# A new plan for a list-scheduled kernel: ScalarE durations from measurement, two row operations on either engine, dummy matmuls in TensorE's gaps

## Chip, cores, metric

One core of a Trainium2 chip. The metric is device microseconds of one execution, median of several runs; a trace's span is about 1.9 us shorter than the time of the same execution (284.2 and 286.15, for one). Engines: PE is TensorE, ACT is ScalarE, DVE is VectorE, POOL is GpSimd, SP issues most DMAs.

## The reference, cut

```python
def _A_ref(q, k, v, shift_k, ssm_k, ssm_D):      # q is layernorm(A_q)
    k_shift = sum(k_pad[:, t:t+S, :] * shift_k[:, ks-1-t] for t in range(ks))   # 4 taps
    kv = k_shift * v
    y = irfft2(rfft2(kv, padded to 2S) * rfft2(ssm_k, padded))[:S]   # causal convolution, length 2048
    return q * (y + kv * ssm_D)
def _B_ref(x, w_gate, w_up, w_down):
    return (silu(x @ w_gate) * (x @ w_up)) @ w_down
x = A_q                                           # [1, 2048, 640], F = 1728
h = x + _A_ref(layernorm(x), A_k, A_v, ...)
return h + _B_ref(layernorm(h), ...)
```

## The kernel before

The sequence is cut into four blocks of 512 rows. For each block, C0 to C3 is the convolution part (taps and gate on DVE, a transform on PE, products with the kernel's transforms G0 to G3 on DVE, the inverse on PE, layernorm on ACT and DVE) and F0 to F3 the FFN. The FFN of block i runs while DVE and ACT prepare block i+1. Every operation is recorded with its engine, a planned duration and what it reads and writes. A list scheduler then fixes the order of each engine's instructions; they are emitted in that order, so the planned times decide nothing but order, engine and buffer. In the views, `ps` is a buffer that matmuls write, and an eviction copies a result out of it (`wgu<-ps`); a statistic sums a row or its squares for a layernorm (`junk<-wk`, `junk<-h`). DELTA is a table of priority offsets, one for each kind of operation.

```python
DELTA = {"C0 ACT half": 5713, "C0 ACT lnh0": 1462, ...}      # 72 entries, cut
def c_act(n): return 0.09 + 0.00078 * n                       # planned ACT time: 0.59 for 640, 1.09 for 1280
def c_mm(n):  return {512: 0.217, 320: 0.137, 128: 0.107}[n]
...
# in Plan.schedule(), for the best ready operation o on engine e, startable at st:
            if e == "PE":
                if st - clock[e] > 2.0:
                    cold = st + 2.6
                if st < cold:                                  # matmuls take twice as long for a while
                    o.dur = 2 * o.dur if ...
...
pl.op("ACT", c_act(2 * D), ... nc.scalar.mul(x.t[:, 2], x.t[:, 2], 0.5), name="half",
      alt=[("DVE", c_ts(2 * D), ...)])                         # halving of a sum lane
pl.op("ACT", c_act(D), ... nc.scalar.activation(h, x, Identity, bias=-mean), name="z",
      alt=[("DVE", 0.356, ...)] if i in LN_EITHER else [])     # LN_EITHER = (0,)
act(c_act(D), ... nc.scalar.activation(hn, h, Identity, bias=..., scale=...), name="hn")   # scaled row, blocks 1 to 3
...
    order = pl.schedule()
    with tc.manual_schedule():
        for o in order:
            o.fn()
```

## Time and profile before

| | before |
|---|---|
| median time | 295.8 us (3 runs, 295.55 to 296.09) |
| span of the trace | 295.6 us |
| busy: PE, DVE, ACT | 259.5, 217.6, 213.3 us |
| first matmul of FFN0 | 68.29 us |
| first matmul of FFN3 | 244.55 us |
| end of the last matmul | 289.3 us |

A busy PE is not PE at its peak, since the ends of pipelined matmuls are modelled; how far the starts of equal matmuls lie apart tells its speed. The prediction below shows views of this trace. To one of its lines a remark: the 4.9 us wait of L809 carries the name of an ACT instruction, but its matmuls read what the gate writes, and the gate ends at 58.7, just before they start:

```profile
57.25 1.48 DVE L775 TENSOR_TENSOR wk<-wk,wk 128x2560 bf16<-128x2560 bf16 x1
```

### The profile page before, as it was taken

The page shows a single profiled execution, that of the slowest core. Times are in us where ns is not written, and L with a number is a line of the kernel's source. Part 1 is how long each engine was busy: PE and PEld are TensorE (multiplying, and loading weights), DVE is VectorE, ACT ScalarE, POOL GpSimd, SP SyncE. Part 2 cuts the span into 40 slices and gives each one's busy share as a digit, 9 for nine tenths or more (in the row PEclk, how much of TensorE's full clock was granted, in tenths as well). Part 3 has the DMA queues.
Part 4 walks back from the last instruction along what each step waited for, and adds up shares of the span by engine and source line. Part 5 has one row for each costly group of instructions (what it writes and reads, how often), then busy time and mean ns, then how long its engine had stood idle before and what let it go on. Part 6 is the DMA issues. An engine that isn't in the chain of part 4 may idle for free.

```text
span 295.6 us, 4242 instructions
## 1 busy us (share of the span) xinstructions
PE 259.5 (88%) x1551; PEld 150.9 (51%) x1564; DVE 217.6 (74%) x300; ACT 213.3 (72%) x377; POOL 31.1 (11%) x38
## 2 busy tenths in 40 slices
PE   3179998388999999899998997999999989999991
PEld 1146766154445576654444665654446754444670
DVE  6994999989989899989998999389999101121111
ACT  3687999979995968998557999962665973545321
POOL 2002001230102023011000030200000011000000
PEclk9999999959999999999999999999999999999998
DMA  7996158992994599935638698864563053550011
GB/s 237 343 376 226 44 232 252 372 385 99 292 347 114 166 351 385 380 112 143 157 71 223 241 323 310 310 214 128 119 173 94 2 133 100 146 133 0 2 44 44
DMA packets 59157, 57.82 MB, mean 196 GB/s; under 512 B 17729, under 2 KB 53762, under 8 KB 59138
## 3 DMA queue, kind: packets, MB, share of 16 engines
q1 hardware_dynamic: 57342, 47.08, 52.3%
q0 software_dynamic: 1792, 10.49, 9.3%
q8 instruction: 12, 0.20, 0.3%
q14 instruction: 7, 0.06, 0.0%
q10 hardware_dynamic: 4, 0.01, 0.0%
HBM read 45.76 MB, written 10.49 MB: 190 GB/s over the span
## 4 chain that ended last, share of the span: by engine, by line
ACT 35%; PE 30%; issue 19%; DVE 7%; DMA 5%; POOL 1%; SPq 1%; POOLq 0%; ACTq 0%; DVEq 0%
PE ps L1009 15%; ACT junk L838 6%; ACT lane L437 5%; PE ps L1033 5%; ACT junk L840 5%; PE ps L792 3%; PE ps L736 3%; ACT s L921 3%; PE ps L809 3%; ACT s L905 3%; DMA wk<-in_A_q_dram 3%; ACT sg L1013 2%; ACT uc L1014 2%; DMA lane<-xd 2%; ACT lane L745 2%
## 5 line engine op out<-in xcount | busy, mean ns | idle before, releaser
L1009 PE MATMUL ps<-hlnT,wgu 128*128 128x512 bf16 x527 | 118.3, 379 | 2.7 <-ACT uc L1014 1.1
L1009 PEld LDWEIGHTS <-wgu 128*128 128x128 bf16 x540 | 52.6, 98 | 66.1 <-issue 4.6
L1013 ACT ACTIVATE sg<-ps 128x512 bf16<-128x512 f32 (+1 forms) x56 | 33.6, 599 | 43.9 <-PE ps L1009 25.4
L1033 PE MATMUL ps<-wdA,tT 128*128 128x320 bf16 x384 | 55.6, 299 | 0.1
L1033 PEld LDWEIGHTS <-tT 128*128 128x128 bf16 x448 | 43.8, 98 | 17.4 <-issue 0.4
L1016 DVE TENSOR_TENSOR tT<-sg,uc 128x512 bf16<-128x512 bf16 (+1 forms) x56 | 22.7, 420 | 38.2 <-ACT uc L1014 38.1
L854 POOL TENSOR_TENSOR mv<-mv,mhalf 128x2 f32<-128x2 f32 (+1 forms) x12 | 18.6, 1551 | 147.2 <-DVE mv L850 81.3
L1014 ACT CAST uc<-ps 128x512 bf16<-128x512 f32 (+1 forms) x56 | 32.7, 584 | 0.3 <-PE ps L1009 0.2
L437 ACT CAST lane<-ps 128x640 bf16<-128x640 f32 x42 | 27.2, 746 | 0.9 <-PE ps L792 0.9
L736 PE MATMUL ps<-wgu,gb_t 128*128 128x320 bf16 x128 | 23.0, 318 | 3.6 <-ACT wgu L672 2.5
L1122 DVE TENSOR_TENSOR lane<-lane,lane 128x3840 bf16<-128x3840 bf16 x12 | 25.8, 2153 | 0.4 <-DMA lane<-xd 0.2
L769 DVE TENSOR_TENSOR wk<-krun,w 128x2560 bf16<-128x2560 bf16 (+1 forms) x20 | 24.0, 1218 | 0.2 <-PE ps L809 0.2
L809 PE MATMUL ps<-wk,cs_t 128*128 128x320 bf16 x96 | 17.3, 326 | 6.8 <-ACT junk L838 4.9
L1038 ACT ACTIVATE o<-ps,mean 128x640 bf16<-128x640 f32 x16 | 12.5, 786 | 14.4 <-PE ps L1033 14.4
L901 PE MATMUL ps<-eo,ci_t 128*128 128x320 bf16 x128 | 18.7, 299 | 1.6 <-DMA wgu<-in_B_w_up_dram 1.0
L736 PEld LDWEIGHTS <-gb_t 128*128 128x128 bf16 x128 | 13.1, 102 | 11.4 <-issue 4.2
L774 DVE TENSOR_TENSOR wk<-wk,wk 128x2560 bf16<-128x2560 bf16 (+1 forms) x15 | 18.0, 1217 | 0.0
L809 PEld LDWEIGHTS <-cs_t 128*128 128x128 bf16 x96 | 9.8, 104 | 12.4 <-DVE wk L775 5.2
L901 PEld LDWEIGHTS <-ci_t 128*128 128x128 bf16 x128 | 12.5, 98 | 7.0 <-issue 1.9
L838 ACT ACTIVATE junk<-wk 128x640 bf16<-128x640 bf16 x16 | 11.9, 747 | 4.6 <-DMA wk<-in_A_q_dram 4.4
L905 ACT ACTIVATE s<-ps,one,mv 128x640 bf16<-128x640 f32 x15 | 13.3, 921 | 1.8 <-POOL mv L854 0.9
L838 ACT ACTIVATE junk<-h 128x640 bf16<-128x640 bf16 x16 | 12.0, 748 | 2.1 <-DVE h L909 1.7
(94 smaller groups left out, 311.9 us busy)
## 6 DMA issues: line engine op xcount, KB each, us to landing
wgu<-in_B_w_gate_dram SPq DMA_DIRECT2D x24, 320.0 KB, 3.4
wgu<-in_B_w_up_dram SPq DMA_DIRECT2D x24, 320.0 KB, 4.3
lane<-xd SPq DMA_DIRECT2D x6, 960.0 KB, 5.5
lane<-hd SPq DMA_DIRECT2D x6, 960.0 KB, 7.9
xd<-lane POOLq DMA_DIRECT2D x4, 960.0 KB, 5.0
hd<-lane POOLq DMA_DIRECT2D x4, 960.0 KB, 6.8
krun<-in_A_k_dram SPq DMA_DIRECT2D x4, 640.0 KB, 6.8
wk<-in_A_v_dram SPq DMA_DIRECT2D x4, 640.0 KB, 8.7
```

Source lines behind the costliest of these rows:

```text
L437: nc.scalar.copy(dst(), src())
L736: nc.tensor.matmul(ps.t[:, h, 0:NH], wt, mv, start=(k == 0), stop=(k == len(ks) - 1))
L769: nc.vector.tensor_mul(dst.t[:, sl, :], ks, w4.t[:, j:j + 1, :].broadcast_to([P, n, D]))
L809: nc.tensor.matmul(ps.t[:, h, 0:NH], cs_t.t[:, s, n, c * P:(c + 1) * P], kv.t[:, s, h * NH:(h + 1) * NH], start=(a == 0), stop=(a == 1))
L838: act(0.73, lambda s=s: nc.scalar.activation(junk.t[:], x.t[:, s, :], ACT.Identity, scale=-1.0 / D, accum_out=mv.t[:, s:s + 1]), [(x, 1 << ...
L901: nc.tensor.matmul(ps.t[:, hh, 0:NH], ci_t.t[:, c, 1 - n, s, :], x.t[:, 2 * pos[n] + c, hh * NH:(hh + 1) * NH], start=(k == 0), stop=(k == 3))
L1009: nc.tensor.matmul(q(ps.t[:, k, 0:w]), wg.t[:, kt, off:off + P], rr(hT.t[:, kt, :]), start=(kt == 0), stop=(kt == NDC - 1))
L1013: act(c_act(w) + 0.02, lambda ps=ps, sg=sg, np_=np_, w=w: nc.scalar.activation(sg.t[0:np_, 0:w], ps.t[0:np_, 0, 0:w], ACT.Silu), [(ps, 1)] ...
L1014: act(c_act(w), lambda ps=ps, uc=uc, np_=np_, lo=up_lo, k=len(offs) - 1, w=w: nc.scalar.copy(uc.t[0:np_, 0:w], ps.t[lo:lo + np_, k, 0:w]), ...
L1016: dve(c_tt(w), lambda sg=sg, uc=uc, c=c, np_=np_, w=w, rr=rr, q=q: nc.vector.tensor_mul(rr(tv()[0:np_, c, :]), q(sg.t[0:np_, 0:w]), q(uc.t ...
L1033: nc.tensor.matmul(ps.t[:, hh, 0:NH], tv()[:, c, m * P:(m + 1) * P], wdc(c)[:, hh * NH:(hh + 1) * NH], start=(c == 0 and not oadd), stop=( ...
L1122: dve(c_tt(6 * D), lambda xl=xl, hl=hl: nc.vector.tensor_mul(xl.t[:], xl.t[:], hl.t[:]), [xl(), hl()], [xl()], name="prod")
```

## The change

Its intent: plan with ACT durations as measured, let the scheduler put two kinds of row operations on either engine in all blocks, fill planned PE gaps after the first 5.5 us with dummy matmuls so that the clock stays up, and use a table of priorities made for that plan.

```diff
-DELTA = {...72 entries...}
+DELTA = {...other entries and values...}
-OPT = (True, (0, 1, 2), (0,), ...)
+OPT = (True, (0, 1, 2), (0, 1, 2, 3), ...)          # LN_EITHER: "z" on either engine in all blocks
             if e == "PE":
-                if st - clock[e] > 2.0:
-                    cold = st + 2.6
+                lo = max(min(since[0], st), clock[e])   # since: when a PSUM buffer is free
+                if lo - clock[e] > 2.5:
+                    cold = st + 4.5
+                gap = st - 0.4 - lo
+                if st < 5.5 or st - clock[e] < 0.8 or gap < 0.3:
+                    o.warm = None
+                else:
+                    slow = min(gap, 5.5) if lo < 6.5 or lo - clock[e] > 2.5 else 0
+                    o.warm = (slots["ps"][since[1]][0], int(slow / 0.44 + (gap - slow) / 0.22))
# durations: half 1.09 -> 1.17, z 0.59 -> 0.72, y 0.59 -> 0.77, hn 0.59 -> 0.812,
#            hT 1.09 -> 1.12, down 0.59 -> 0.677; some DVE ones too
-                    act(c_act(D), ... name="hn")
+                    act(0.812, ... name="hn",
+                        alt=[("DVE", 0.357, ... nc.vector.tensor_scalar(hn, h, mean, rstd, op0=ALU.add, op1=ALU.mult))])
         for o in order:
+            if o.warm:
+                for _ in range(o.warm[1]):
+                    nc.tensor.matmul(o.warm[0][:, 0, :], ones1.t[:], ones1.t[:].unsqueeze(1).broadcast_to([P, 4, P]), start=True, stop=True)
             o.fn()
```

More of the change, by code (lines that the diff above doesn't have):

```diff
@@ L30 @@
 DELTA = {
-    "C0 ACT half": 5713,
-    "C0 ACT lnh0": 1462,
-    "C0 ACT y": 1339,
-    "C0 ACT z": -2549,
-    "C0 DVE eo0": -2261,
-    "C0 DVE gate": -16818,
-    "C0 DVE prod0": -14678,
-    "C0 DVE tinyx": 31,
-    "C0 PE inv0": -2297,
-    "C0 SP ci_t": 16022,
-    "C0 SP cs_t": 3931,
-    "C0 SP gb_t": 1107,
-    "C0 SP k": -728,
-    "C0 SP v": -11,
-    "C0 SP x": -2141,
-    "C1 ACT hn": 2424,
-    "C1 ACT xev1": -969,
-    "C1 ACT y": -4984,
-    "C1 DVE bfly0": -24238,
-    "C1 DVE bfly1": -22972,
@@ L51 @@
-    "C1 DVE eo0": -3933,
-    "C1 DVE eo1": -21519,
-    "C1 DVE hmul0": -24066,
-    "C1 DVE hmul1": -17335,
-    "C1 DVE join0": -4523,
-    "C1 DVE last": -3933,
-    "C1 DVE nm": -14579,
-    "C1 DVE prod": 733,
-    "C1 DVE tinyh1": -3279,
-    "C1 DVE xsum0": -3000,
-    "C1 PE hTtr": -11983,
-    "C2 ACT hn": -6262,
-    "C2 DVE eo0": -12365,
-    "C2 DVE eo1": -13863,
-    "C2 DVE gate": -18349,
-    "C2 DVE hmul0": -4317,
-    "C2 DVE join0": -14364,
-    "C2 DVE last": -99,
-    "C2 DVE nm": 22411,
@@ L70 @@
-    "C2 DVE prod": -4774,
-    "C2 DVE tinyx": -180,
-    "C2 DVE xsum0": -668,
-    "C2 DVE xsum1": -2435,
-    "C3 ACT hn": -8326,
-    "C3 ACT lnh0": 10,
-    "C3 ACT lnh1": -9704,
-    "C3 DVE bfly1": 20,
-    "C3 DVE comb": 3729,
-    "C3 DVE psum": -4522,
-    "C3 DVE shift": 2173,
-    "C3 DVE xsum1": 3949,
-    "C3 PE x1": -26875,
-    "C3 SP ldX": -5040,
-    "F0 DVE ffn": -3823,
-    "F0 PE down": 1944,
-    "F0 SP w": 1894,
-    "F1 PE down": 3501,
-    "F2 DVE ffn": 2826,
-    "G0 ACT gev": -234,
@@ L90 @@
-    "G0 DVE g_fold": -2452,
-    "G0 DVE skip": -2446,
-    "G0 PE g_transform": -10973,
-    "G1 ACT gev": 13784,
-    "G1 ACT half": 1293,
-    "G1 DVE g_fold": -5018,
-    "G2 ACT gev": 14649,
-    "G2 DVE g_sum": 2060,
-    "G2 PE g_turn_pe": 6402,
-    "G3 DVE g_fold": -1695,
-    "G3 DVE g_sum": 2144,
-    "G3 PE g_transform": -6565,
-    "slack SP": 3733,
+    "C0 ACT half": 860,
+    "C0 ACT lnx": 4481,
+    "C0 ACT z": 3190,
+    "C0 DVE comb": -22511,
+    "C0 DVE eo0": -12858,
+    "C0 DVE g_sum": -1393,
@@ new lines @@
+    "C0 DVE gate": -4264,
+    "C0 DVE hmul1": -12868,
+    "C0 DVE hn": -12782,
+    "C0 DVE prod0": -22408,
+    "C0 DVE shift": 4071,
+    "C0 DVE tinyx": -13190,
+    "C0 DVE xsum1": -22414,
+    "C0 SP gst": -15574,
+    "C0 SP k": -29642,
+    "C0 SP v": -16164,
+    "C0 SP x": -16163,
+    "C1 ACT lnh1": 10,
+    "C1 ACT xev0": 2001,
+    "C1 DVE bfly1": -35167,
+    "C1 DVE comb": -5098,
+    "C1 DVE eo0": -5103,
+    "C1 DVE gate": -13467,
+    "C1 DVE hmul0": -29485,
+    "C1 DVE last": -35177,
@@ new lines @@
+    "C1 DVE shift": -13857,
+    "C1 DVE tinyx": -4494,
+    "C1 DVE xsum0": -31182,
+    "C2 ACT lnh0": 1661,
+    "C2 DVE bfly1": -26086,
+    "C2 DVE hmul0": -23662,
+    "C2 DVE join1": -23656,
+    "C2 DVE shift": 177,
+    "C2 DVE tinyh0": -1588,
+    "C2 DVE tinyh1": -2274,
+    "C2 POOL powh0": -1915,
+    "C2 SP ldH": 3496,
+    "C3 ACT lnx": -2040,
+    "C3 ACT y": -2113,
+    "C3 DVE bfly0": -280,
+    "C3 DVE bfly1": -277,
+    "C3 DVE comb": -307,
+    "C3 DVE join0": -8105,
+    "C3 DVE last": -307,
@@ new lines @@
+    "C3 DVE prod": -331,
+    "C3 DVE psum": -1636,
+    "C3 DVE xsum0": -283,
+    "C3 DVE xsum1": -612,
+    "F0 ACT down": 826,
+    "F0 ACT ffn": -95114,
+    "F0 DVE ffn": -4711,
+    "F1 ACT down": -17057,
+    "F1 PE down": 8902,
+    "F2 ACT down": 993,
+    "F2 ACT ffn": -5061,
+    "F2 DVE ffn": -177,
+    "G0 ACT turn": -3610,
+    "G0 PE g_transform": -610,
+    "G1 ACT half": -914,
+    "G1 DVE g_sum": -12920,
+    "G1 SP gst": 4770,
+    "G2 ACT gev": 1247,
+    "G2 ACT half": -34281,
@@ L103 @@
+    "G2 DVE g_fold": -1451,
+    "G2 DVE g_sum": 1031,
+    "G2 PE g_turn_pe": 11630,
+    "G3 ACT half": -11180,
+    "G3 DVE g_fold": -27113,
+    "G3 DVE g_sum": -2044,
+    "G3 PE g_transform": -94287,
+    "slack ACT": 4,
+    "slack SP": 954,
 }
-OPT = (True, (0, 1, 2), (0,), (), (0, 1, 2), (1, 2, 3), True, (0,), (0,), 0, (0, 1, 2))
+OPT = (True, (0, 1, 2), (0, 1, 2, 3), (), (0, 1, 2), (1, 2, 3), True, (0,), (0,), 0, (0, 1, 2))
 def bf(a):
@@ L175 @@
 class Op:
-    __slots__ = ("i", "eng", "dur", "fn", "deps", "succ", "allocs", "frees", "pri", "nwait", "ready", "soft", "alts", "key", "start", "end", "tag", "nbytes", "fix")
+    __slots__ = ("i", "eng", "dur", "fn", "deps", "succ", "allocs", "frees", "pri", "nwait", "ready", "soft", "alts", "key", "start", "end", "tag", "nbytes", "fix", "warm")
 class Plan:
@@ L213, in op @@
         o.pri += DELTA.get(o.key, 0)
-        o.deps, o.succ, o.soft, o.allocs, o.frees = set(), [], [], [], []
+        o.deps, o.succ, o.soft, o.allocs, o.frees, o.warm = set(), [], [], [], [], None
         for x, wr in [(x, False) for x in r] + [(x, True) for x in w] + [((b, 0), True) for b in alloc]:
@@ L297, in schedule @@
             o.eng, o.dur, o.fn = next(x for x in o.alts if x[0] == e)
+            since = min(free["ps"], default=(st, 0))
             for b in o.allocs:
@@ L744, in g_sum @@
             dve(c_tt(2 * D), lambda x=x: nc.vector.tensor_add(x.t[:, 2], x.t[:, 0], x.t[:, 1]), [x(15)], [x(48)])
-            pl.op("ACT", c_act(2 * D), lambda x=x: nc.scalar.mul(x.t[:, 2], x.t[:, 2], 0.5), [x(48)], [x(48)], name="half",
+            pl.op("ACT", 1.17, lambda x=x: nc.scalar.mul(x.t[:, 2], x.t[:, 2], 0.5), [x(48)], [x(48)], name="half",
                   alt=[("DVE", c_ts(2 * D), lambda x=x: nc.vector.tensor_scalar_mul(x.t[:, 2], x.t[:, 2], 0.5))])
@@ L886, in back @@
         for s in range(NS):
-            pl.op("ACT", c_act(D), lambda s=s: nc.scalar.activation(h.t[:, s, :], xt.t[:, s, :], ACT.Identity, bias=mvx.t[:, s:s + 1]),
+            pl.op("ACT", 0.72, lambda s=s: nc.scalar.activation(h.t[:, s, :], xt.t[:, s, :], ACT.Identity, bias=mvx.t[:, s:s + 1]),
                   [(xt, 1 << s), (mvx, 1 << s)], [(h, 1 << s)],
-                  alt=[("DVE", 0.356, lambda s=s: nc.vector.tensor_scalar_add(h.t[:, s, :], xt.t[:, s, :], mvx.t[:, s:s + 1]))] if i in LN_EITHER else [], name="z")
+                  alt=[("DVE", 0.296, lambda s=s: nc.vector.tensor_scalar_add(h.t[:, s, :], xt.t[:, s, :], mvx.t[:, s:s + 1]))] if i in LN_EITHER else [], name="z")
         mvs = []
@@ L903, in back @@
                 pe(8 * c_mm(320), mm, [ci_t, (src[r][0], 15)], [ps], alloc=[y], name=f"inv{r}")
-                pl.op("ACT", c_act(D), lambda y=y, a=a, s=s, ps=ps: nc.scalar.activation(v2(y.t[:, a, :]), r3(ps.t), ACT.Identity, bias=one.t[:], scale=mvx.t[:, NS + s:NS + s + 1]),
+                pl.op("ACT", 0.77, lambda y=y, a=a, s=s, ps=ps: nc.scalar.activation(v2(y.t[:, a, :]), r3(ps.t), ACT.Identity, bias=one.t[:], scale=mvx.t[:, NS + s:NS + s + 1]),
                       [ps, one, (mvx, 16 << s)], [(y, 1 << a)],
-                      alt=[("DVE", 0.74, lambda y=y, a=a, s=s, ps=ps: nc.vector.tensor_scalar(v2(y.t[:, a, :]), r3(ps.t), mvx.t[:, NS + s:NS + s + 1], 1.0, op0=ALU.mult, op1=ALU.add))] if i == 0 else [], name="y")
+                      alt=[("DVE", 0.8, lambda y=y, a=a, s=s, ps=ps: nc.vector.tensor_scalar(v2(y.t[:, a, :]), r3(ps.t), mvx.t[:, NS + s:NS + s + 1], 1.0, op0=ALU.mult, op1=ALU.add))] if i == 0 else [], name="y")
             sl, m = slice(r, NS, 2), 5 << r
@@ L916, in nm @@
                     nc.vector.tensor_mul(mv.t[:, 3 * NS + r:4 * NS:2], mv.t[:, r:NS:2], mv.t[:, NS + r:2 * NS:2])
-                dve(0.13, nm, [(mvs[r], 5 * 17 << r)], [(mvs[r], 5 * 4096 << r)], name="nm")
+                dve(0.08, nm, [(mvs[r], 5 * 17 << r)], [(mvs[r], 5 * 4096 << r)], name="nm")
             for a in range(2):
@@ L920, in back @@
                 if i in HN_ACT:
-                    act(c_act(D), lambda hn=hn, a=a, s=s, mv=mvs[r]: nc.scalar.activation(hn.t[:, a, :], h.t[:, s, :], ACT.Identity, bias=mv.t[:, 3 * NS + s:3 * NS + s + 1], scale=mv.t[:, NS + s:NS + s + 1]),
-                        [(h, 1 << s), (mvs[r], 4112 << s)], [(hn, 1 << a)], name="hn")
+                    act(0.812, lambda hn=hn, a=a, s=s, mv=mvs[r]: nc.scalar.activation(hn.t[:, a, :], h.t[:, s, :], ACT.Identity, bias=mv.t[:, 3 * NS + s:3 * NS + s + 1], scale=mv.t[:, NS + s:NS + s + 1]),
+                        [(h, 1 << s), (mvs[r], 4113 << s)], [(hn, 1 << a)], name="hn",
+                        alt=[("DVE", 0.357, lambda hn=hn, a=a, s=s, mv=mvs[r]: nc.vector.tensor_scalar(hn.t[:, a, :], h.t[:, s, :], mv.t[:, s:s + 1], mv.t[:, NS + s:NS + s + 1],
+                                                                                                     op0=ALU.add, op1=ALU.mult))])
                 else:
@@ L943, in turned @@
                     return ps.t[:].bitcast(BF16)[:, :, 0:D].rearrange("p a (k t) -> p a k t", k=NDC)
-                pl.op("ACT", c_act(2 * D), lambda dst=dst, src=turned: nc.scalar.copy(dst(), src()), [ps], [(hT, 5 << r)],
-                      alt=[("DVE", 0.8, lambda dst=dst, src=turned: nc.vector.tensor_copy(dst(), src()))], name="hT")
+                pl.op("ACT", 1.12, lambda dst=dst, src=turned: nc.scalar.copy(dst(), src()), [ps], [(hT, 5 << r)],
+                      alt=[("DVE", 0.742, lambda dst=dst, src=turned: nc.vector.tensor_copy(dst(), src()))], name="hT")
         return h, hT
@@ L1037, in ffn @@
                 with pl.at(EVAC[i]):
-                    act(c_act(D), lambda ps=ps, m=m: nc.scalar.activation(v2(o.t[:, m, :]), r3(ps.t), ACT.Identity, bias=mean[f"x{i}"].t[:, m:m + 1]), [ps, mean[f"x{i}"]], [(o, 1 << m)], name="down")
+                    act(0.677, lambda ps=ps, m=m: nc.scalar.activation(v2(o.t[:, m, :]), r3(ps.t), ACT.Identity, bias=mean[f"x{i}"].t[:, m:m + 1]), [ps, mean[f"x{i}"]], [(o, 1 << m)], name="down")
             with pl.at(EVAC[i]):
```

## The prediction

> **What bounds the kernel now.** I first read the busy time by stretch, cut where TensorE (PE) changes its character.
>
> ```profile
> 13.80:18.20 4.40, 2.32 (x21) 2.12 (x22) 4.37 (x8) 4.31 (x10) 0.00 (x0) 1.00 1.12 341
> 18.20:24.20 6.00, 6.00 (x24) 3.33 (x24) 4.16 (x11) 4.05 (x5) 0.00 (x0) 1.00 1.05 395
> 24.30:53.90 29.60, 27.84 (x218) 19.33 (x215) 27.40 (x36) 28.26 (x39) 3.86 (x5) 1.00 0.56 187
> 53.90:68.30 14.40, 8.48 (x54) 5.47 (x54) 12.84 (x17) 12.42 (x24) 4.37 (x2) 0.76 0.95 346
> 68.30:245.30 177.00, 168.56 (x991) 95.95 (x1001) 149.98 (x195) 139.77 (x259) 19.74 (x22) 1.00 0.66 203
> 245.30:289.40 44.10, 43.82 (x243) 23.65 (x242) 6.76 (x15) 17.56 (x32) 0.69 (x2) 1.00 0.27 71
> ```
>
> After the stretch and its length come PE, weight loads, VectorE (DVE), ScalarE (ACT) and GpSimd, then the clock and the DMA share. From 68.3 us, where the first FFN (FFN0) starts, PE is the bound: its idle pieces in the timeline to 289.3 add to 7.4 us. Before that it is not: from 24 to 68 us ACT and DVE are both about 90% busy (28.26 and 27.40 of 29.6, then 12.42 and 12.84 of 14.4), and PE waits. After 289.3 come 6.3 us of eviction, add and store, which the change leaves alone.
>
> Next the waits of PE, and the timeline, for how fast its matmuls ran.
>
> ```profile
> PE ps L670 <- DVE wk L702: 8.8, 1, 8.8
> PE ps L809 <- ACT junk L838: 4.9, 1, 4.9
> PE ps L736 <- ACT wgu L672: 2.5, 2, 2.1
> ```
>
> ```profile
> 18.95 0.74 PE L736 MATMUL ps<-wgu,gb_t 128*128 128x320 bf16 x2
> 19.48 0.47 PE L736 MATMUL ps<-o,ones 128*128 128x320 bf16 x1
> ...
> 25.42 2.34 PE L736 MATMUL ps<-wgu,gb_t 128*128 128x320 bf16 x16
> ...
> 60.88 3.36 PE L809 MATMUL ps<-wk,cs_t 128*128 128x320 bf16 x12 [0.84 <-ACT lane L437]
> ```
>
> Three matmuls every 0.80 us at 19 us is 0.27 us each; sixteen in 2.2 us at 25.4 is 0.136. PE runs at half speed until about 24 us, and again from 58.8 to about 65, after the 4.9 us hole. (The clock column shows 1.00 in the first stretch, so there the durations are the evidence.)
>
> A floor follows from the counts and warm pitches of the timeline. From FFN0's first matmul on PE owes 540 matmuls of 512 columns at 0.223 us (29.30 us for 132), 664 of 320 columns at 0.137 and 40 transposes at 0.06: 120.2 + 91.0 + 2.4 = 213.6 us. The span is then 68.3 (start of FFN0) + 213.6 + 7.4 (gaps) + 6.3 (tail) = 295.6, as measured. The 213.6 and 6.3 stay; the start of FFN0 and the gaps can move.
>
> **What the Trainium skill says.** (1) "TensorE: Matmul & The Clock Gate", Part 1: PE's clock is half until about 3.4 us of activity, and an idle window of that length halves it again. The trace agrees on the factor (0.27 against 0.136) and that the 4.9 us hole cools it; the warm-up took longer here, 5.7 us of dense work from 18.2 us. (2) "ScalarE: Activation LUTs", What ACT_TABLE_LOAD costs: an ACTIVATE takes 186 ns + 0.833 ns per column, about 93 ns more for each pointer operand, and neighbours overlap by about 93. For 640 columns and two pointers that is 905 ns, pitch 812; the trace has 916 for the scaled rows (L921), two starting 0.81 apart. (3) Same page, Rules for kernel authors: simple arithmetic belongs on VectorE, up to about 3 times faster in bf16. The trace agrees:
>
> ```profile
> L921 ACT ACTIVATE s<-h,mv 128x640 bf16<-128x640 bf16 x12 | 10.4, 916 | 0.0
> L924 DVE TENSOR_SCALAR s<-h,mv 128x640 bf16<-128x640 bf16 x4 | 1.5, 444 | 0.6 <-POOL mv L854 0.6
> L745 ACT ACTIVATE h<-h 128x1280 bf16<-128x1280 bf16 x2 | 2.6, 1283 | 0.0
> L746 DVE TENSOR_SCALAR lane<-lane 128x1280 bf16<-128x1280 bf16 x1 | 0.5, 494 | 0.0
> ```
>
> **The change part by part.** Most of it is data for a list scheduler: durations and priorities decide order and engine. So I read the built order. The old plan had ACT at 0.59 us for a 640-wide row that costs 0.72 to 0.81 in pitch, and 1.09 for a halving that costs 1.16; the new figures match the trace. Real matmuls and bytes are the same.
>
> *a) Fill matmuls.* 38 dummy 512-wide matmuls: 28 after the first eight matmuls, 10 ahead of the first transposes of FFN0's input. The 28 start at 5.1 us. If the clock opens after 5.7 us, as it did from 18.2, 13 run at 0.427 and 15 at 0.216, to about 14: where L670 starts anyway (13.8). At most a few tenths are lost and not on the path. The gain: L670's 20 transposes take 1.2 instead of 2.2 us, L736's first 24 matmuls 3.3 instead of 6.3. The later 10 (2.2 us) keep the clock up over the hole, where about 3 us were lost to half speed.
>
> *b) ACT's order at the start.* Now only six statistics stand ahead of the eviction of the kernel transposes, not eight, at 0.86 us each: it ends at 10.17 + 6 x 0.86 + 1.16 = 16.5 instead of 18.2. Both G0 halvings go from ACT to DVE (0.43 each instead of 1.16). Walking ACT's order by pitches (0.59 eviction, 0.73 row, 0.86 statistic, 1.16 double eviction, 1.06 negation) the last eviction of the first X transform ends near 31, not 36.2.
>
> *c) DVE to FFN0.* To 19.1 us nothing changes. Then skip and both further folds come early, in time in which DVE idled 3.8 us waiting for cold L736. With pitches 0.735 (1280 wide), 1.405 (2560), 2.07 (3840): second product's end 35.4, first two eo 40.0, second hmul 52.6, gate 56.2. The chain closes through ACT: its four last statistics end near 56.5, small operations, power and GpSimd take to 59, a product to 59.1, two rows at 0.36 to 59.8 (before: 64.0), transposes to 60.6, another product, then the eviction on DVE at 62.6. FFN0 starts near 63. ACT arrives after its table load at 65; four PSUM buffers of 2.2 us each hide that, while before PE stood 0.9 us at 72.8. I add 0.5 for semaphore delays that pitches omit: 63.5, a gain of 4.8.
>
> *d) Scaled rows on either engine.* Eleven instead of four rows on DVE: seven times 0.81 off ACT, 2.5 us onto DVE. For block 3 (three rows on DVE) the rows go straight after GpSimd's power (234.2 and 237.6 in the old trace) instead of behind statistics (236.4 and 239.4). They feed serial DMA transposes of 1.4 us each, and FFN3's 0.8 us wait for the last should vanish.
>
> *e) Boundary gaps.* The new PE order no longer interleaves block 1's transform between down projections: one run of 32 matmuls, then 115 of FFN1. Walking FFN0 from 63, the join before the second inverse ends 2 us early, but the gate that releases the 32 matmuls ends only 0.4 us before PE wants it. I put the gaps after FFN0's start at 4.0 instead of 7.4: two thirds of the small ACT-caused waits go, some come back at that gate.
>
> Sum: 63.5 + 213.6 + 4.0 + 6.3 = 287.4 us, 2.8% less. The fill's savings are inside the 63.5, not added again, since ACT and DVE bind there.
>
> **Rivals.** *Rival 1: the front gain is real but DVE gives it back.* By my count of its instructions DVE owes 53 us in a 56.5 us FFN0 period, and it was busy 150 of 177 us from 68.3 on; the change adds about 1 us net (rows 2.5 and two halvings, less evictions). If block 1's gate or the joins slip 2 to 3 us, gaps go to 7 or 8: 291. Against it: DVE idles longer in FFN2 (10.24 of 20 us busy at 220 to 240), and old DVE work can be pushed there. *Rival 2: dummy matmuls delay real ones.* If the clock opened only near 13 us, the 28 would take until 15.9; the 10 also need a free PSUM buffer and stand ahead of the transposes. That costs up to 2 us in front: 289. For it: in-order PE; against it: the 1.4 us before ACT is free at 15.4. *Rival 3: PE's warm speed counts in full* and ACT and DVE keep up: FFN0 at 61.5, gaps 2: 283.4. Against it: ACT is booked solid from 31 to 65 in my walk. *Rival 4: nothing moves,* because another wait (a DMA, since the third ssm-kernel load and the second now come later) holds the front: the second kernel load should land about 17 to 18 us by the bytes ahead of it, needed at 19.5. Small risk.
>
> **Range and chances.** FFN0's start is good to about 2 us and the gaps to about 3, partly shared; that gives 283.5 to 292. The 2% line lies at 289.9, 2.5 us above my number and about a standard deviation away less a little: faster 0.75, same 0.24, slower 0.01.
>
> **What would show it.** Right: L736's first 24 matmuls at 0.137 each, not 0.27; L670 still at 13.8 to 14.5; no stretch of half speed near 60; last scaled rows of block 0 on DVE near 60 and FFN0's first matmul at 63 to 64; PE's idle time after that near 4 us; FFN3 with no wait for a DMA. Wrong: FFN0 still at 66 or later (my ACT walk omitted a wait), or a new PE wait of over 2 us on DVE ahead of block 1's transform, or dummy matmuls still running when the transposes are ready.

## The result

| | before | after |
|---|---|---|
| median time | 295.94 us (4 runs) | 286.39 us (4 runs, 286.15 to 286.54) |
| span of the trace | 295.6 | 284.2 |
| first matmul of FFN0 | 68.29 | 61.95 |
| first matmul of FFN3 | 244.55 | 233.19 |
| listed idle pieces of PE from FFN0 on | 7.4 | 3.4 |
| from the last matmul to the end | 6.3 | 6.3 |

The ratio is 0.9663 (95% interval 0.9618 to 0.9708). Ratios here are the mean time of one kernel's fast runs over that of the other's of the same rounds, so not quite the ratio of the medians quoted. A caution on the traces: the profiled execution of before took 297.4 us, 1.5 more than its median, so the 11.4 us between the two spans is more than the 9.6 us between the medians.

Busy time by stretch of the changed kernel (columns as in the prediction), cut at FFN0 and near FFN3:

```profile
13.80:62.00 48.20, 41.22 (x323) 28.18 (x324) 47.22 (x71) 47.06 (x77) 8.33 (x7) 1.00 0.85 298
62.00:238.00 176.00, 171.66 (x1009) 97.74 (x1020) 152.99 (x203) 136.62 (x255) 19.84 (x22) 1.00 0.67 206
238.00:278.00 40.00, 39.75 (x224) 21.86 (x224) 6.35 (x14) 16.16 (x30) 0.54 (x1) 1.00 0.27 69
```

In the first stretch DVE (47.22 of 48.20) and ACT (47.06) are now busy 98%: the front is still theirs, but hardly a gap is left in it. After that PE is the bound, as before.

The waits of PE and some of its timeline in the changed kernel:

```profile
PE ps L745 <- ACT s L914: 3.3, 2, 2.0
PE ps L679 <- DVE wk L711: 1.4, 1, 1.4
PE ps L818 <- DVE wk L784: 0.9, 1, 0.9
PE ps L1020 <- DMA hlnT<-s: 0.5, 1, 0.5
```

```profile
4.56 7.96 PE L1170 MATMUL ps<-ones 128*128 128x512 bf16 x28
13.96 0.73 PE L679 MATMUL ps<-ident,wk 128*128 128x128 bf16 x10 [1.44 <-DVE wk L711]
...
16.69 0.43 PE L745 MATMUL ps<-wgu,gb_t 128*128 128x320 bf16 x2
16.96 0.30 PE L745 MATMUL ps<-o,ones 128*128 128x320 bf16 x1
17.10 0.43 PE L745 MATMUL ps<-wgu,gb_t 128*128 128x320 bf16 x2
...
51.56 2.32 PE L1170 MATMUL ps<-ones 128*128 128x512 bf16 x10
...
61.95 4.48 PE L1020 MATMUL ps<-hlnT,wgu 128*128 128x512 bf16 x19 [0.51 <-DVE hlnT L956]
```

L745 is the old L736. Three of its matmuls start every 0.41 us: 0.137 each, full speed. The 28 dummies end at 12.5, ahead of the transposes. The 8.8 us wait of before has become dummy work and 1.4 us. The 4.9 us wait has become dummy work, 0.9 us behind it and 2.0 us ahead of it, where the last four L745 now wait for ACT: the longer of the two pieces of 3.3 us, the largest listed wait of the changed kernel.

### The profile page after: what moved, and what is told of

The parts are those of the page before. It is cut to its first block, busy times and chain, and to the rows that moved or that the text cites.

```text
span 284.2 us, 4320 instructions
## 1 busy us (share of the span) xinstructions
PE 262.9 (93%) x1589; PEld 151.7 (53%) x1602; DVE 218.6 (77%) x306; ACT 207.0 (73%) x371; POOL 31.2 (11%) x38
## 4 chain that ended last, share of the span: by engine, by line
PE 30%; DVE 24%; issue 21%; ACT 17%; DMA 3%; POOL 3%; SPq 0%; POOLq 0%; DVEq 0%; ACTq 0%
PE ps L1020 17%; PE ps L1044 8%; ACT lane L446 3%; PE ps L910 3%; DVE lane L1133 3%; DVE wk L778 3%; POOL mv L863 3%; DVE wk L783 2%; ACT junk L847 2%; DMA krun<-in_A_k_dram 2%; ACT s L914 2%; ACT junk L849 2%; PE ps L818 2%; DVE lane L874 1%; DMA lane<-xd 1%
## 5 line engine op out<-in xcount | busy, mean ns | idle before, releaser
L1133 DVE TENSOR_TENSOR lane<-lane,lane 128x3840 bf16<-128x3840 bf16 x12 | 25.8, 2152 | 2.2 <-DMA lane<-hd 2.2
L745 PE MATMUL ps<-wgu,gb_t 128*128 128x320 bf16 x128 | 20.8, 298 | 4.5 <-ACT s L914 3.3
L1049 ACT ACTIVATE o<-ps,mean 128x640 bf16<-128x640 f32 x16 | 12.5, 786 | 16.0 <-PE ps L1044 16.0
L745 PEld LDWEIGHTS <-gb_t 128*128 128x128 bf16 x128 | 12.3, 97 | 11.2 <-issue 5.6
L818 PE MATMUL ps<-wk,cs_t 128*128 128x320 bf16 x96 | 14.7, 298 | 1.8 <-DVE wk L784 0.9
L914 ACT ACTIVATE s<-ps,one,mv 128x640 bf16<-128x640 f32 x16 | 13.9, 896 | 3.0 <-POOL mv L863 2.0
L910 PEld LDWEIGHTS <-ci_t 128*128 128x128 bf16 x128 | 12.5, 98 | 5.5 <-issue 0.4
L1137 DVE TENSOR_TENSOR lane<-lane,lane 128x3840 bf16<-128x3840 bf16 x6 | 12.9, 2152 | 0.0
```

The source lines that it names most:

```text
L745: nc.tensor.matmul(ps.t[:, h, 0:NH], wt, mv, start=(k == 0), stop=(k == len(ks) - 1))
L910: nc.tensor.matmul(ps.t[:, hh, 0:NH], ci_t.t[:, c, 1 - n, s, :], x.t[:, 2 * pos[n] + c, hh * NH:(hh + 1) * NH], start=(k == 0), stop=(k == 3))
L1133: dve(c_tt(6 * D), lambda xl=xl, hl=hl: nc.vector.tensor_mul(xl.t[:], xl.t[:], hl.t[:]), [xl(), hl()], [xl()], name="prod")
```

## The experiments

e1, e2, e4 and e9 keep the changed order and undo one thing; e3 adds one thing to the old order. FFN0 times are of the profiled execution of each. All runs gave correct results, and all figures are of fast runs; two of e6's four runs were slow and are left out. The runs stand on three chips (e1 to e4, e5 to e8, e9 to e12), on which before took 296.44, 295.49 and 296.48 us. So a loss against the changed kernel is taken from ratios to before and given as a range, against e5's 0.9698 and against the result's 0.9663 (0.001 is 0.3 us).

**e5: the changed kernel again**, as a control on the chip of e6 to e8.

> The changed kernel again, as the control on the chip of these runs: 286 to 287 us, FFN0 from 62 to 63 us in the profile, and L745 warm if the 28 dummies hold the clock there (in the run with the 28 alone they did not).

286.71 us (286.53 to 287.22), ratio to before 0.9698; FFN0 at 62.48, L745 warm. The result stands.

**e1 and e2: no dummies, or the early 28 alone.**

```diff
-            if o.warm:
+            if False:                       # e1
+            if o.warm and o.warm[1] > 20:   # e2
```

> The changed order with none of the 38 dummy matmuls; nothing else differs. Theory (VectorE and ScalarE bind before FFN0, so a cold TensorE is partly hidden): L745's first 24 matmuls at half speed again, ending about 3 us later; ScalarE loses about 2 us of it, FFN0 starts 2 to 3 us later than 61.95, some more if the clock also falls near 55 us: 288.3 to 290 us against 286.4. Rival (the front gain of 6 us is mostly the warm clock): FFN0 back at 66 or later, 291 us or more. Second rival (dummies cost about what they save): 286 to 287.

> The changed order with the 28 early dummies but without the 10 ahead of block 0's transposes. Theory: the first half is as in the changed kernel; the idle pieces near 51 to 55 us (2.2 and 0.9 us around ten transposes) may let the clock fall, then L818's 24 matmuls take up to twice as long but the second scaled rows end only at 59.0: FFN0 0 to 1.5 us later, 286.4 to 288. Rival (the clock near 60 us was worth the 3 us lost to half speed in the old kernel): 289 or more.

e1: 287.9 us (287.71 to 288.83), ratio 0.9715. e2: 288.08 us (287.19 to 288.93), ratio 0.9723. All 38 dummies are worth 0.5 to 1.5 us, less than the 1.9 to 3.6 of my theory and far from the rival's 5; the intervals of the ratios overlap the control's. FFN0 starts at 63.54 in e1 and 64.36 in e2: of the 6.3 us by which FFN0 came earlier, 4.8 remain without any dummy. PE's timeline in e1 shows the hole without its ten dummies:

```profile
52.57 0.70 PE L745 MATMUL ps<-wgu,gb_t 128*128 128x320 bf16 x4 [1.96 <-ACT s L914]
55.19 1.25 PE L947 MATMUL ps<-ident,s 128*128 128x128 bf16 x10 [1.92 <-DVE s L935]
56.94 4.99 PE L818 MATMUL ps<-wk,cs_t 128*128 128x320 bf16 x24 [0.51 <-DVE wk L784]
```

Ten transposes take 1.25 us instead of 0.72 and L818's 24 matmuls 4.99: half speed at first (the granted clock reads 0.50 from 53.35 to 60.18), though no listed idle piece is longer than 1.96 us. It costs little, because the next transposes wait for the scaled rows anyway: they start at 61.77 instead of 59.55, and 1.6 of those 2.2 us are e1's lateness ahead of the hole (L745 at 52.57 instead of 50.97). In e2's profiled execution the clock was lost even behind the 28 dummies:

```profile
5.03 8.68 PE L1170 MATMUL ps<-ones 128*128 128x512 bf16 x28
14.98 0.73 PE L679 MATMUL ps<-ident,wk 128*128 128x128 bf16 x10 [1.27 <-DVE wk L711]
16.00 0.73 PE L679 MATMUL ps<-ident,wk 128*128 128x128 bf16 x10 [0.29 <-ACT junk L849]
17.14 0.69 PE L745 MATMUL ps<-wgu,gb_t 128*128 128x320 bf16 x2 [0.41 <-ACT wgu L681]
17.63 0.47 PE L745 MATMUL ps<-o,ones 128*128 128x320 bf16 x1
```

The transposes ran at full speed but L745 started at half. Up to here e2 has the same instructions as the changed kernel, whose two traces, and those of e4 and e9, show L745 warm; so this differs from execution to execution (why, the clock records suggest: see the last section). The early dummies are a likely gain, not a sure one, and what e2 loses cannot be put down to the ten missing dummies alone.

**e3: the old order with dummies**, 28 ahead of L670 and 16 ahead of the first L809.

```diff
+        fill = {"G0 PE g_turn_pe": 28, "C1 PE x0": 16}
         for o in order:
+            for _ in range(fill.pop(o.key, 0)):
+                ps = next(x for x in o.allocs if x.cls == "ps")
+                nc.tensor.matmul(ps.t[:, 0, :], ones1.t[:], ...)
             o.fn()
```

> The old order and old plan with 28 dummies ahead of L670 and 16 ahead of the first L809; nothing else differs. Theory: L736 runs warm, ScalarE gets back most of the 2.3 us it waited for L736 between 19 and 25 us, VectorE its 3.8 us; the rest of the front is bound by ScalarE and VectorE: gain 1.5 to 3 us of the 9.6, so 293 to 294.5. Rival (warm clock is the gain): 5 us or more, 291 or less.

294.45 us against 296.44 of before in the same rounds (ratio 0.9938, 0.9894 to 0.9981): 2 us, as the theory said. L736 is warm, the first X transform ends about 3 us earlier, FFN0 starts at 65.72. Dummies alone are thus a fifth of the gain in the old order. The 16 later ones did not hold the clock: it reads 0.50 from 57.05 to 63.88.

**e4: the seven scaled rows of blocks 2 and 3 back on ACT**, in the same place of the order.

```diff
+            if o.key in ('C2 ACT hn', 'C3 ACT hn'):
+                o.fn = o.alts[0][2]
             o.fn()
```

> The changed order with the seven scaled rows of blocks 2 and 3 that VectorE took put back on ScalarE at the same place in the order. Theory: block 3's first two rows delay its last statistics by about 1.6 us and with them the last transposes by DMA, so FFN3 starts 1.5 to 2 us later; block 2's four rows add 3.2 us to ScalarE's queue ahead of FFN2, 0 to 1 us of it seen: 288 to 289. Rival (the rows' engine is off the critical path, only the planned order matters): 286.4 within 0.5.

292.65 us (290.77 to 293.31), ratio 0.9867: 5 to 6 us are lost, more than twice what I expected. Ahead of FFN2, in e4:

```profile
173.26 0.44 PE L947 MATMUL ps<-ident,s 128*128 128x128 bf16 x5
174.31 0.45 PE L947 MATMUL ps<-ident,s 128*128 128x128 bf16 x5 [0.61 <-ACT s L930]
175.12 0.45 PE L947 MATMUL ps<-ident,s 128*128 128x128 bf16 x5 [0.36 <-ACT s L930]
176.66 0.45 PE L947 MATMUL ps<-ident,s 128*128 128x128 bf16 x5 [1.08 <-ACT s L930]
178.05 0.69 PE L1041 MATMUL ps<-h,ident 128*128 128x320 bf16 x2 [0.94 <-ACT o L1049]
178.54 4.58 PE L1044 MATMUL ps<-wdA,tT 128*128 128x320 bf16 x24
182.96 0.71 PE L1044 MATMUL ps<-wdB,tT 128*128 128x320 bf16 x4
```

and in the changed kernel:

```profile
172.99 1.28 PE L947 MATMUL ps<-ident,s 128*128 128x128 bf16 x20
174.96 0.43 PE L1041 MATMUL ps<-h,ident 128*128 128x320 bf16 x2 [0.69 <-ACT o L1049]
175.23 3.42 PE L1044 MATMUL ps<-wdA,tT 128*128 128x320 bf16 x24
178.49 0.71 PE L1044 MATMUL ps<-wdB,tT 128*128 128x320 bf16 x4
```

Each row now stands behind statistics in ACT's queue, and the transposes come in four pieces. PE's idle pieces add to 0.61 + 0.36 + 1.08 + 0.94 = 3.0 us instead of 0.7, and the 24 matmuls behind them take 4.42 us instead of 3.26, because the clock fell (it reads 0.50 from 177.48 to 180.89). FFN2 starts at 183.50 instead of 179.11; 0.3 of these 4.4 us were there at FFN0. FFN3 starts 6.2 us late, so block 3 adds 1.8: that part was as expected. The rows are worth 5 to 6 us *in this order*; what they are worth once the scheduler may plan anew, e12 asks.

**e9: the two G0 halvings back on ACT.**

```diff
+            if o.key == 'C0 ACT half':
+                o.fn = o.alts[0][2]
             o.fn()
```

> The changed order with the two G0 halvings put back on ScalarE (1.16 us each) from VectorE (0.43 each) at the same place. My prediction counted them as part of what frees ScalarE before 31 us. Theory: FFN0 starts about 1 us later, 287.2 to 288. Rival (VectorE alone binds the front in the changed kernel: it is busy from 5 to 62 us with little idle time): nothing, or 0.5 us less, 286 to 286.9.

288.17 us (287.99 to 288.79), ratio 0.9727: 0.9 to 1.9 us over the changed kernel, where the theory had 0.8 to 1.5. PE's timeline shows why:

```profile
29.57 0.70 PE L801 MATMUL ps<-wk,cs_t 128*128 128x320 bf16 x4 [1.88 <-ACT lane L446]
```

ACT evicts the X transform too late by almost the full 2 x 1.16 us, and nothing later takes it up: FFN0 starts at 64.23. So ACT binds the front up to 31 us, as the prediction's (b) had it. The rival, DVE alone, is out.

**e6, e7, e8: the table of priorities.** e6 is the changed code with the old table, e7 and e8 are the changed and the old code with an empty one.

```diff
-DELTA = {...}
+DELTA = {...the old table...}   # e6
+DELTA = {}                      # e7 (changed code), e8 (old code)
```

> All of the changed code (measured times, alternatives, dummies) but the old table of priorities, so the order is planned anew. Theory (the times and alternatives carry most of the gain, the table only refines it): 288 to 291. Rival (the gain is the new table, found for this model; an old table that was found for other times fits no better than none): 294 or more.

> The changed code with an empty table of priorities. Theory (times and alternatives): 5 to 9 us under the old code with an empty table (e8), some 290 to 296 in all. Rival (the table): within 3 us of e8, both 297 or more.

> The old code with an empty table. Both theories expect more than 296: some 298 to 303. It is the partner of e7; the difference of the two is what measured times, alternatives and dummies give without a searched table.

| | old code | changed code |
|---|---|---|
| empty table | 328.04 (e8) | 318.36 (e7) |
| old table | 295.49 (before) | 304.14 (e6, mean of two fast runs: 302.53 and 305.75) |
| new table | not run | 286.71 (e5) |

My theory for e6 falls: the old table in the changed code is 8 us slower than the old kernel (ratio 1.0284). A table fits the code for which it was made (whether the durations or the alternatives matter, e6 does not tell); each table is worth about 32 us to its own code (328.0 to 295.5, 318.4 to 286.7). Without a table the changed code gains 9.7 us and with its own 8.8, which looked as if times, alternatives and dummies carried the whole gain. But e8 has waits of 15.8, 13.2 and 12.1 us on PE and a mean clock of 0.931; its 9.7 us need not be the same 9 us. In size my expectations for both runs missed: I gave 290 to 296 for e7 and 298 to 303 for e8.

**e10, e11, e12: new searches on the planner.** A plan needs no chip, so priorities can be searched without one. I set the planner's matmul times to the measured ones (0.2226 for 512 columns, 0.062 for 128), since 540 matmuls at 0.217 hide 3 us, and ran random searches of 50 minutes on the planner's own span: with all of the change (e10, best of four), with the old ACT times (e11, best of two), with measured times but without the new alternatives (e12, best of two).

```diff
-        return {512: 0.217, 320: 0.137, 128: 0.107}[n]
+        return {512: 0.2226, 320: 0.137, 128: 0.062}[n]    # all three, each with its own searched DELTA
# e11: z, y, hn, down back to c_act(D), half and hT to c_act(2 * D), nm, and DVE's z, y and hT to the old figures
# e12: LN_EITHER = (0,), "hn" without its alternative
```

> The changed code with the planner's matmul times set to the measured ones (0.2226 us for 512 columns, 0.062 for 128) and a table of priorities searched anew for that (best of four searches of 50 minutes). The planner's own span is 282.9 where the changed order would be about 284.1 by the same times. Theory (a plan with measured times comes true): 284.5 to 286.5, so up to 2 us better than the changed kernel. Rival (the searched table fits the plan's remaining errors): 287 or more.

> As e10, but planned with the old ScalarE times (0.59 for rows, 1.09 for the 1280-wide ones) and searched anew (best of two searches of 50 minutes); its own span is 280.3, better than e10's. Theory (the measured times are what makes the plan come true): the chip takes longer than for e10 by 4 us or more, 289 to 295. Rival (alternatives and dummies are the gain, the times do not matter): within 1.5 us of e10.

> As e10, with the measured times but without the new alternatives: FFN inputs of blocks 1 to 3 on ScalarE alone for the x minus mean rows, and their scaled rows on ScalarE alone, searched anew (best of two searches of 50 minutes); its own span is 283.3. Theory (times first, alternatives second): within 2 us above e10, 285 to 288. Rival (e4 showed 6 us for seven rows: the alternatives are the larger part): 290 or more.

| | planner's span | median on the chip (range) | ratio to before | FFN0 | FFN3 |
|---|---|---|---|---|---|
| e10, all | 282.9 | 290.51 (288.54 to 291.63) | 0.9792 | 61.39 | 237.40 |
| e11, old ACT times | 280.3 | 288.70 (288.17 to 292.18) | 0.9766 | 62.89 | 235.40 |
| e12, no alternatives | 283.3 | 291.80 (290.51 to 293.20) | 0.9847 | 58.13 | 238.05 |
| changed kernel (time of e5, FFN0 and FFN3 of the first trace) | about 284.1 | 286.71 (286.53 to 287.22) | 0.9698 | 61.95 | 233.19 |

None beats the changed kernel, against my expectation for e10 (284.5 to 286.5); its rival, a table fitted to the plan's remaining errors, gave 287 or more. e12 missed as well (285 to 288). All three beat the old kernel by 4.7 to 7.8 us. They differ by 3.1 us; of each setting only the best plan was run, so what chance in the search does is not known, and e10 had four searches where the others had two. So:

- That measured ACT times make the difference is *not* shown: e11, planned with the old ones, is not slower than e10.
- The alternatives, worth 5 to 6 us in the fixed order of e4, are worth 1.3 us, within the ranges, once the order is planned without them. The scheduler had other ways. (Nearly all of this freedom is in the scaled rows: 11 instead of 4 are on DVE, but of the rows "z" three are on DVE before, L889, and three after, L898.)
- The planner's span ranked two good plans wrongly: e10's was 1.2 us better than that of the changed order and its time 3.8 us worse (2.8 by the ratios). It loses this after FFN0: from FFN0 to FFN3 e10 takes 176.0 us and the changed kernel 171.2. The largest of its waits:

```profile
PE ps L1164 <- ACT uc L1169: 3.5, 3, 2.7
PE ps L682 <- DMA hlnT<-in_A_shift_k_dram: 2.3, 1, 2.3
PE ps L889 <- ACT wgu L825: 1.4, 2, 0.8
```

The first counts 3.5 us in three waits, the longest 2.7; in the changed kernel the same kind adds to 1.5. Behind that longest wait the clock fell too: it reads 0.50 from 214.37 to 217.78. e10's two fastest runs of six (288.54 and 288.69) have the highest mean clocks, 0.995 and 0.994, so part of what it loses differs from execution to execution.

## Why the prediction was right, point by point

**The sum.** Predicted: FFN0 at 63.5, work 213.6, gaps 4.0, tail 6.3. The trace: 61.95; 216.0 from there to the last matmul, of which 3.4 are listed idle pieces, so 212.6; and 6.3. The mechanism was right: the start of FFN0 and the gaps moved. (The work is 1.0 us under the 213.6 for the same matmuls; most of that is rounding, since 16 matmuls of 320 columns take 2.17 us, 0.1356 each, and 664 of them at 0.137 are 0.9 us too many.) In the trace the sum came out 3.2 us too high, half of it in the first term: I added 0.5 us for semaphores, but all steps came 0.7 to 1 us earlier than I walked them. Against the *time* it was only 1.0 us too high, because I set the span equal to the time, where the time is 1.9 us longer. Two errors of opposite sign thus cancel in part: that closeness is luck.

**(a) Dummies.** The warm matmuls came as predicted (L745 at 0.137 each). "Not added again, since ACT and DVE bind there" was right in kind and too strict in size: without them 0.5 to 1.5 us are lost, not none.

**(b) ACT's order and the halvings.** Walked: the kernel's eviction ends at 16.5 and the X transform's at 31. The trace has L745 starting at 16.3 and the last eviction ending at 31.3. e9 confirms that ACT is the limit there.

**(c) DVE's chain.** Walked: rows at 59.8, eviction 62.6, FFN0 near 63. In DVE's timeline of the changed kernel:

```profile
58.29 0.80 DVE L935 TENSOR_SCALAR s<-h,mv 128x640 bf16<-128x640 bf16 x2 [0.59 <-POOL mv L863]
59.01 2.15 DVE L1133 TENSOR_TENSOR lane<-lane,lane 128x3840 bf16<-128x3840 bf16 x1
61.08 0.81 DVE L956 COPY hlnT<-ps 128x1280 bf16<-128x1280 bf16 x1
```

Rows end at 59.1, then the product, then the eviction at 61.9: the chain as predicted.

**(d) Scaled rows.** For block 3 right: 1.8 us in e4 against a prediction that FFN3's wait would go; a rest of 0.5 us stayed. For block 2 the prediction gave no figure and e4's expectation said 0 to 1 us: here the size was wrong, about 4 us in the fixed order. What I missed is that a row behind statistics delays PE in pieces, and that these pieces take the clock down.

**(e) Gaps.** 3.4 listed against 4.0 predicted. The gate that I saw as tight, 0.4 us, was: the matmuls behind it start at 114.52, about 0.1 us after PE is free.

**The rivals.** DVE did not give the gain back (rival 1); the 28 dummies were over at 12.5 (13.6 in e4, the slowest), before the transposes (rival 2). Rival 3 came nearer in number than the prediction: it said FFN0 at 61.5, gaps of 2 and 283.4, and the trace has 61.95, 3.4 and a span of 284.2. The warm speed that it counted in full is not most of the gain, since FFN0 starts at 63.54 with no dummy at all (e1); the prediction, which gave 63.5 with the dummies counted in, hit what the kernel does without them. Rival 4 is out: from FFN0 on, PE's only listed wait for a DMA is 0.5 us. Of the signs set down for being right, two did not come true: FFN0 at 63 to 64, and no DMA wait at FFN3 (0.47 us remain).

**What stays open:** why this table of priorities beats the searched ones by 2 to 5 us. The planner, with the measured times, ranks it behind them (284.1 against 282.9 and 283.3). Whether it was chosen with times from the chip, the change does not say, and no run here shows it. Also open: the front gains 4.8 us without dummies, of which e9 explains about 2 (its FFN0 is at 64.23); the rest was walked in the prediction, not tested by a run.

## What to carry to other kernels

Where a scheduler makes the order, split the trace where the binding engine changes and ask of each part whose queue ends it: 6.3 of the 11.4 us between the two traces came from the stretch before PE binds, in part by taking small operations out of a full ACT queue (e9). Undoing one choice in a fixed order tells what that order rests on, not what the choice is worth; plan anew before crediting it. A priority table is part of the model it was found with, and a plan's own span need not rank good plans rightly (here two that were 1.2 us apart): those must be run.

## What the Trainium skill lacked or had wrong

- "TensorE: Matmul & The Clock Gate", Part 1 (warm-up about 3.4 us of activity, plus or minus 0.5, with a warning that it varies): in five traces of this front order the 28 dummies start 0.425 us apart at first and 0.215 later, and the change comes 3.0 to 5.7 us behind their start; before took 5.9 us from 18.2. The spread is wider than 0.5. What the same part says of a free-running window of 3413 ns does agree: within each trace the changes of the granted clock lie whole multiples of 3.41 us apart (24.10, 58.24 and 65.06 in before; 10.04, 16.87 and 20.28 in e2). So the same gap may or may not cool the clock, by where it falls; that would explain e2, though no run tests it.
- Same page, the rule of no idle gap over about 3 us: here the clock fell with no listed idle piece over 1.96 us (e1 at 53.35; PE was busy 1.37 us of the 3.41 before) and in e4 at 177.48 (1.36 of 3.42), among four pieces of 0.4 to 1.1 us. It held in the changed kernel behind 3.4 us with 1.53 and 1.72 busy (from 49.08 and from 11.53), and fell in e2 behind 1.71. In these traces the busy share of such a stretch tells more than the longest gap, but no sharp limit comes out.
- Same page, Part 4 (transposes do not count as PE activity as matmuls do, and the full clock does not engage for them): no run settles the first half, since behind the same 20 transposes the clock fell in e2 and held in four other traces. The second half, read as the speed of transposes, does not hold: 20 transposes took 1.28 us at full speed, 10 took 1.25 at half.
- "ScalarE: Activation LUTs" does not give the price of an ACTIVATE with an accumulator: here 0.74 us for 640 columns and 0.19 for reading the accumulator, and 0.86 from one to the next, where a row without it (and with a bias operand) takes 0.72 from one to the next.
- No page says that the granted-clock column can read 1.00 while matmuls run at half speed, as in the first 24 us of before (0.27 us for 320 columns). The trace holds no clock record before 24.10, and the view counts time without a record as full; later the two agree (0.50 from 58.24 to 65.06). So at the start of a trace the durations decide.
